# The last row of wo: sixteen DMAs of 15 rows down to 1 in place of one DMA of 128 rows

## The chip, the cores and the metric

The kernel runs on one core of a Trainium2 chip. Its five engines are named as in the profile: PE (TensorE, with PEld for its weight loads), DVE (VectorE), ACT (ScalarE), POOL (GpSimd) and SP (SyncE), beside 16 DMA engines that move data between HBM and SBUF. The metric is device time in microseconds (us) of one execution, lower is better, given as the median of several runs. Beside it there is a profile of one execution: a page, and a trace that can be asked for more.

## The reference, cut to what matters

One decoding step of a layer for 8 sequences: attention over a key and value cache, and beside it an MLP, both from the same normalised input, summed with the input.

```python
# B=8, Sq=1, D=640, Hq=Hkv=32, Sk=4096, Dh=128, F=1728; all bfloat16
def _A_ref(x, k_cache, v_cache, wq, wo):
    q = transpose((x @ wq).reshape(B, Sq, Hq, Dh), 0, 2, 1, 3)
    scores = jnp.einsum("bhqd,bhkd->bhqk", q, k_cache) * (Dh ** -0.5)
    p = _softmax(scores, axis=-1)
    o = jnp.einsum("bhqk,bhkd->bhqd", p, v_cache)
    return transpose(o, 0, 2, 1, 3).reshape(B, Sq, Hq * Dh) @ wo

def _B_ref(x, w1, b1, w2, b2):
    y = _layernorm(x)
    h = _gelu(jnp.einsum("bsd,df->bsf", y, w1) + b1)
    return jnp.einsum("bsf,fd->bsd", h, w2) + b2

xn = _layernorm(A_x)
return A_x + _A_ref(xn, ...) + _B_ref(xn, ...)
```

The two caches are 8 x 32 x 4096 x 128 elements of two bytes each, 268 MB apiece; the page counts 551.80 MB read from HBM in all. wo has 4096 rows (32 heads of 128) of 640 columns.

## The kernel before

The attention is done in 32 turns (`NQ`), one for each sequence and each group of 8 heads (`HS`). A turn loads 8 heads of the key cache and 8 of the value cache, 8 MB each, as 128 partitions with 256 keys of 128 elements. A part of the scores is computed by DVE (multiply, add, reduce), the rest by transposes and matmuls on PE; ACT does the exponentials and PE the product with V. K goes alternately to two slots of one large SBUF tensor (`S_sb`), V to a third.

Each engine's program is written down by hand: `at(pos, fn, ...)` gives every step a position, the steps are sorted by it, and each engine's calls are recorded in that order. `_Eng` records compute instructions with a semaphore, and `_Dma` counts 16 on its semaphore for each DMA, so that `sig` hands back a ticket of the semaphore and the sum so far. `_Eng.wait` waits for a ticket. On PE, DVE and ACT the turns run as loops; SP's program has no loop.

SP issues all large loads in order: wq, then K and V turn by turn, the MLP's weights w1 and w2, and at the end wo. x, b2, the rest of w2, b1 and the final store are issued by ACT. Nearly everything in the core's stream from HBM thus stands in one queue, in SP's order.

wo is loaded last, because its place in SBUF is the slot of the last odd turn's K: `load_wl` (line 382) waits until that K has been read. Its five DMAs follow one another without another wait. `load_wl(0)` brings the first half (20 KB for each partition), `load_wl(1)` the third quarter (10 KB), and `load_wn` (line 395) the last quarter in three pieces, cut at `WN_CUT = (0, 5, 7, HS)` (line 230): five of the eight rows that each partition holds, then two, then one. In the prediction these are `wn0`, `wn1` and `wn2`. A piece of one row is 640 elements, 1280 bytes, on each of 128 partitions: partition p gets row 8p + 7 of the last 1024 rows of wo. Each piece has a semaphore of its own (`ld_wn`).

At the end PE multiplies the attention output by wo into ACC_ps, an accumulator that already holds x, b2 and the MLP's result. `fin_wl` does it for the first three quarters. `fin_wn(q)` (line 766) waits for its piece of the last quarter and for the reordered output of the last heads (`oS3_sb`), and then runs five matmuls for each of its rows: 25, 10 and 5. `fin_store` (line 777) waits for the last matmul, copies ACC_ps to SBUF on DVE, transposes it on PE, evicts it on ACT and issues the store from ACT. SP's last instruction waits for that store.

The recorded instructions all go out through the helper `_emit`, so the profile gives nearly all of them line 111, and its waits line 109.

Of the kernel before, what the change touches and what calls it, by code (L numbers as in the profile page):

```python
# [14 lines left out]
P = 128  # L15
# [177 lines left out]
def bass_parallel_sum__gqa_block_cached__mixer_channel_mlp__decode_kernel(  # L193
# [13 lines left out]
    B, _, D = A_x.shape  # L207
# [3 lines left out]
    HS = 8  # L211
# [16 lines left out]
    RW = P // HW  # L228
    NL = 3
    WN_CUT = (0, 5, 7, HS)  # L230
    V_CUT = (0, 192, 256)

    def jp_of(i):
# [17 lines left out]
    with ExitStack() as es:  # L251
# [7 lines left out]
        def part(slot, lo, n, rows=P):  # L259
            return S_sb[0:rows, slot, lo:lo + n]  # L260
# [3 lines left out]
        def scratch(n, rows=P, slot=KB):  # L264
# [14 lines left out]
        woL_sb = part(KB, HW * D, 2 * HS * D).rearrange("p (g x) -> p g x", g=2)  # L279
# [58 lines left out]
        pe, dve, act, sp, pool = (_Eng(sem(f"{n}_s")) for n in ("pe", "dve", "act", "sp", "pool"))  # L338
# [3 lines left out]
            _Dma(sem(n)) for n in ("ld_x", "ld_b1", "ld_b2", "ld_wq", "ld_w1", "ld_w2a", "ld_w2b", "st_o"))  # L342
        ld_vl = [_Dma(sem(f"ld_vl{q}")) for q in range(1, len(V_CUT) - 1)]
        ld_wl = [_Dma(sem(f"ld_wl{q}")) for q in range(2)]
        ld_wn = [_Dma(sem(f"ld_wn{q}")) for q in range(len(WN_CUT) - 1)]
        tk = {}
        prog = []

        def at(pos, fn, *a):
            prog.append((pos, len(prog), fn, a))  # L350
# [21 lines left out]
        def load_v(i):  # L372
# [4 lines left out]
            tk[("v", i)] = []  # L377
            for d, lo, hi in zip([ld_s[VS]] + ld_vl, V_CUT[:-1], V_CUT[1:]):
                if lo:
# [15 lines left out]
        def load_wn(q):  # L395
            lo, hi = WN_CUT[q], WN_CUT[q + 1]
            n = HS * DH
            tk[("wn", q)] = ld_wn[q].sig(sp.dma_start(
                woL_sb[:, 1, lo * D:hi * D],
                A_wo[NL * n:(NL + 1) * n, :].rearrange("(p s) n -> p (s n)", p=P)[:, lo * D:hi * D]))  # L400

        def zero_w2b():
            tk["w2z"] = pool.sig(pool.memset(w2b_sb[:, :], 0.0))
# [264 lines left out]
        def pe_PV(i):  # L668
            PVB.use(pe)
            pe.wait(tk[("exp", i)])  # L670
            for j in range(NKEY):
                if j == 0:
                    pe.wait(tk[("v", i)][0])
                elif j in V_CUT:
                    pe.wait_ge(ld_vl[V_CUT.index(j) - 1].sem, 1)
                last = pe.matmul(PV_ps[:, 0:HS], tile[VS][:, j, :], P_sb[:, :, j],
# [89 lines left out]
        def fin_wn(q):  # L766
            lo, hi = WN_CUT[q], WN_CUT[q + 1]
            pe.wait(tk[("wn", q)], tk[("oS", 3, 0)], tk[("oS", 3, 1)])
            for r in range(lo, hi):
                for c in range(DC):  # L770
                    last = pe.matmul(ACC_ps[:, c * B:(c + 1) * B],
                                     woL_sb[:, 1, r * D + c * P:r * D + (c + 1) * P], oS3_sb[:, r, :],
                                     start=False, stop=(r == HS - 1), skip_group_check=True)
            if hi == HS:
                ACCB.used(pe, pe.sig(last))
# [73 lines left out]
        for q in range(2):  # L849
            at(o + 50 + 0.1 * q, load_wl, q)  # L850
            at(o + 79.1 + 0.2 * q, fin_wl, q)
        for q in range(len(WN_CUT) - 1):
            at(o + 51 + q, load_wn, q)
            at(o + 80 + q, fin_wn, q)
# [70 lines left out]
```

## Time and profile before

| | |
|---|---|
| Time, median of 3 runs | 1281.99 us (1281.98 to 1282.0) |
| Span of the profiled execution, first to last instruction | 1280.5 us |
| Busy: DVE | 1103.8 us (86%) |
| Busy: PE | 671.1 us (52%) |
| Busy: PE's weight loads | 573.4 us (45%) |
| Busy: ACT | 476.6 us (37%) |
| Busy: POOL | 106.3 us (8%) |
| HBM traffic over the span | 431 GB/s |
| Issue of the five DMAs of wo on SP | from 1255.97 us, 2.23 us in all |

The median is 1.5 us above the span, for what lies before the first and after the last instruction. Busy times are instruction records; the issue of a DMA, a wait and a branch do not count as busy. Times in rows are microseconds from the start of the span. The DMA row gives the busy share of the 16 DMA engines together, in tenths; "DMA share" in a table of windows is the same as a fraction. The queue q1 is SP's and q10 is ACT's; a "packet" is one record of a DMA engine, either data or the small write that reports completion. "SPq" and "ACTq" stand for the issue of a DMA by that engine.

### The profile page before, as it was taken

What the parts mean: (1) busy time and instruction counts of PE and PEld (TensorE: products, weight loads), DVE (VectorE), ACT (ScalarE), POOL (GpSimd) and SP (SyncE); (2) the same over time, 40 slices, a digit from 0 to 9 for tenths busy, and PEclk for the clock granted to TensorE, in tenths of its full rate; (3) what the DMA queues carried; (4) which work ended last, traced back from release to release, by engine and by line L of the source; (5) the groups of instructions that cost most, each with busy time, mean ns of one, the idle gap of its engine ahead of it and who ended that gap; (6) DMA issues with size and microseconds to landing.
All of it is one profiled execution on the core that took longest, in us unless ns stands there. A gap on an engine that the chain in (4) does not pass through costs nothing.

```text
span 1280.5 us, 34440 instructions
## 1 busy us (share of the span) xinstructions
PE 671.1 (52%) x13944; PEld 573.4 (45%) x13944; DVE 1103.8 (86%) x680; ACT 476.6 (37%) x904; POOL 106.3 (8%) x113
## 2 busy tenths in 40 slices
PE   1546555446545446545456554456454466464476
PEld 1435444335535345444345444345343355353365
DVE  1899999889888889888899888898888898888895
ACT  0524444233444233443234443234443234442331
POOL 0020010000000000000000000000000000000040
PEclk9755655566665565555565565566655555555655
DMA  9999999999999999999999999999999999999998
GB/s 419 431 426 435 426 436 432 442 426 436 432 440 428 434 432 438 432 432 430 436 438 426 434 434 442 426 434 434 438 430 430 430 440 436 428 432 436 433 437 361
DMA packets 10675, 551.99 MB, mean 431 GB/s; under 512 B 1244, under 2 KB 1445, under 8 KB 1702
## 3 DMA queue, kind: packets, MB, share of 16 engines
q1 hardware_dynamic: 10512, 551.70, 99.7%
q8 instruction: 9, 0.15, 0.0%
q10 hardware_dynamic: 150, 0.11, 0.0%
q14 instruction: 4, 0.03, 0.0%
HBM read 551.80 MB, written 0.01 MB: 431 GB/s over the span
## 4 chain that ended last, share of the span: by engine, by line
DMA 52%; DVE 36%; issue 11%; DVEq 0%; PE 0%; SPq 0%; ACT 0%
DMA S_sb<-in_A_k_cache_dram 51%; DVE S_sb L111 26%; DVE Sd_sb L111 8%; DMA S_sb<-in_A_wo_dram 2%; DVE S_ps L111 1%; DVE ri_sb L111 0%; DVEq L109 0%; PE ACC_ps L111 0%; DVE mx_sb L111 0%; SPq L111 0%; DVE mbT_sb L111 0%; DVE mxT_sb L111 0%; DVE mq_sb L111 0%; DVE mb_sb L111 0%; PE QB_ps L111 0%
## 5 line engine op out<-in xcount | busy, mean ns | idle before, releaser
L111 PE MATMUL TR_ps<-ident_bf,S_sb 128*128 128x128 bf16 (+1 forms) x2570 | 341.2, 273 | 354.1 <-POOL kr_sb L111 333.7
L111 DVE TENSOR_TENSOR S_sb<-S_sb,qbc_sb 128x7552 bf16<-128x7552 bf16 (+1 forms) x96 | 392.5, 4088 | 128.8 <-DMA S_sb<-in_A_k_cache_dram 128.4
L111 PEld LDWEIGHTS TR_ps<-ident_bf,S_sb 128*128 (+2 forms) x2570 | 243.6, 102 | 414.0 <-issue 338.2
L111 DVE TENSOR_REDUCE Sd_sb<-S_sb 128x59 f32<-128x3776 bf16 (+1 forms) x96 | 390.2, 4065 | 6.0
L111 ACT ACTIVATE KT_sb<-TR_ps 128x1024 bf16<-128x1024 bf16 x320 | 327.0, 1024 | 121.1 <-PE TR_ps L111 109.5
L111 PE MATMUL PV_ps<-P_sb,S_sb 128*128 128x8 bf16 x8192 | 224.0, 175 | 137.5 <-DMA S_sb<-in_A_v_cache_dram 134.5
L111 PEld LDWEIGHTS PV_ps<-P_sb,S_sb 128*128 128x128 bf16 x8192 | 221.4, 103 | 140.2 <-DMA S_sb<-in_A_v_cache_dram 137.0
L111 DVE TENSOR_TENSOR S_sb<-S_sb 128x3776 bf16<-128x3776 bf16 (+1 forms) x96 | 205.4, 2140 | 3.3
L111 ACT ACTIVATE P_sb<-Sd_sb,NB_sb 128x256 bf16<-128x256 f32 x256 | 126.3, 494 | 213.7 <-DVE NB_sb L111 213.7
L111 PE MATMUL S_ps<-qrep_sb,KT_sb 128*128 128x8 bf16 x2560 | 121.6, 177 | 51.6 <-ACT KT_sb L111 48.6
L111 ACT ACTIVATE oU_sb<-PV_ps 128x8 f32<-128x8 f32 x31 | 5.5, 178 | 376.8 <-PE PV_ps L111 376.8
L111 PEld LDWEIGHTS S_ps<-qrep_sb,KT_sb 128*128 128x128 bf16 x2560 | 91.3, 102 | 82.2 <-ACT KT_sb L111 41.6
L111 POOL TENSOR_TENSOR oT_sb<-oU_sb,ri_sb 128x8 bf16<-128x8 f32 x31 | 71.8, 2316 | 374.8 <-DVE S_sb L111 303.1
L111 POOL COPY qrep_sb<-qT_sb 128x128 bf16<-128x128 bf16 x32 | 19.2, 600 | 472.6 <-PE S_ps L111 454.0
L111 ACT ACTIVATION_READ_ACCUMULATOR P_sb<-Sd_sb,NB_sb 128x1 f32 x256 | 47.7, 186 | 0.0
L111 DVE TENSOR_TENSOR S_ps<-S_ps,mask_sb 128x320 f32<-128x320 f32 (+1 forms) x65 | 31.6, 486 | 2.6 <-PE S_ps L111 2.6
L111 DVE TENSOR_REDUCE Sd_sb<-S_ps 128x40 f32<-128x320 f32 x64 | 31.5, 492 | 2.2
L111 PE MATMUL QB_ps<-ident_bf,qrep_sb 128*128 128x128 bf16 x32 | 9.2, 286 | 40.7 <-DVE S_sb L111 21.2
L111 ACT ACTIVATE qbc_sb<-QB_ps 128x128 bf16<-128x128 f32 x32 | 8.9, 278 | 56.9 <-PE QB_ps L111 56.9
L111 POOL MEMSET kr_sb<- 128x1 f32 x32 | 3.2, 99 | 295.4 <-DMA S_sb<-in_A_k_cache_dram 295.4
L111 PEld LDWEIGHTS QB_ps<-ident_bf,qrep_sb 128*128 128x128 bf16 x32 | 3.3, 104 | 43.6 <-ACT oU_sb L111 29.3
L111 PE MATMUL CH_ps<-rs_sb,ones_f 128*128 128x8 f32 x64 | 16.7, 335 | 6.5 <-ACT P_sb L111 6.5
(73 smaller groups left out, 148.6 us busy)
## 6 DMA issues: line engine op xcount, KB each, us to landing
S_sb<-in_A_v_cache_dram SPq DMA_DIRECT2D x1, 6144.0 KB, 26.8
S_sb<-in_A_wq_dram SPq DMA_DIRECT2D x1, 5120.0 KB, 15.2
S_sb<-in_A_wo_dram SPq DMA_DIRECT2D x1, 2560.0 KB, 15.8
S_sb<-in_B_w_dram SPq DMA_DIRECT2D x1, 2160.0 KB, 30.3
S_sb<-in_B_w_dram SPq DMA_DIRECT2D x1, 2080.0 KB, 34.8
S_sb<-in_A_v_cache_dram SPq DMA_DIRECT2D x1, 2048.0 KB, 31.3
S_sb<-in_A_wo_dram SPq DMA_DIRECT2D x1, 1280.0 KB, 18.5
S_sb<-in_A_wo_dram SPq DMA_DIRECT2D x1, 800.0 KB, 20.0
```

Of the source, the lines that this page charges most:

```text
L111: inst = getattr(e, name)(*a, **k)
```

## The change

`load_wn` is changed for the piece that reaches the last row (`hi == HS`, that is `wn2`). Instead of one DMA to 128 partitions it issues sixteen, each to the next k partitions, with k from a new list, `ROWS_CUT`: 15, 14, 13, 12, 11, 10, 9, 8, 8, 7, 6, 5, 4, 3, 2, 1, which add up to 128. The other two pieces keep their one DMA of 128 partitions. Each of the sixteen adds 16 to the same semaphore; the ticket kept is that of the last, so PE's wait in `fin_wn(2)` is for 256 instead of 16. The bytes, their source and their place are the same.

```diff
     WN_CUT = (0, 5, 7, HS)
+    ROWS_CUT = (15, 14, 13, 12, 11, 10, 9, 8, 8, 7, 6, 5, 4, 3, 2, 1)
     V_CUT = (0, 192, 256)
...
         def load_wn(q):
             lo, hi = WN_CUT[q], WN_CUT[q + 1]
             n = HS * DH
-            tk[("wn", q)] = ld_wn[q].sig(sp.dma_start(
-                woL_sb[:, 1, lo * D:hi * D],
-                A_wo[NL * n:(NL + 1) * n, :].rearrange("(p s) n -> p (s n)", p=P)[:, lo * D:hi * D]))
+            src = A_wo[NL * n:(NL + 1) * n, :].rearrange("(p s) n -> p (s n)", p=P)
+            a = 0
+            for k in ROWS_CUT if hi == HS else (P,):
+                tk[("wn", q)] = ld_wn[q].sig(sp.dma_start(
+                    woL_sb[a:a + k, 1, lo * D:hi * D], src[a:a + k, lo * D:hi * D]))
+                a += k
```

On PE, DVE, ACT and POOL the program is the same. On SP one DMA of 128 x 640 elements, the last one of its queue, becomes sixteen.

## The prediction

> **What bounds the kernel now.** I read the page's busy lines first, then the chain that ended last, then its last pieces in order of time.
>
> ```profile
> span 1280.5 us, 34440 instructions
> DMA  9999999999999999999999999999999999999998
> HBM read 551.80 MB, written 0.01 MB: 431 GB/s over the span
> DMA 52%; DVE 36%; issue 11%; DVEq 0%; PE 0%; SPq 0%; ACT 0%
> ```
>
> The DMA engines are busy in every slice and the core draws 431 GB/s throughout. The kernel is a stream from HBM; the change adds no byte and moves none to an earlier place, so only the end of the stream can matter. The last pieces of the chain of waits:
>
> ```profile
> 1255.97 0.33 SPq L111
> 1256.30 0.04 issue
> 1256.34 0.43 SPq L111
> 1256.77 0.04 issue
> 1256.82 19.96 DMA S_sb<-in_A_wo_dram
> 1276.78 0.05 issue
> 1276.82 1.50 PE ACC_ps L111 x40
> 1278.33 0.02 issue
> 1278.35 0.21 DVE res_sb L111
> ```
>
> The end hangs on wo: from 1276.82 PE runs 40 matmuls into ACC_ps, then the result is copied, transposed, evicted and stored. The 40 are three groups behind three waits: 25 for the first piece of wo's last eighth (`wn0`), 10 for the second (`wn1`), 5 for the third (`wn2`, the edited DMA). Windows laid on the gaps, with the instructions that touch ACC_ps alone, show each wait (columns: stretch, length, PE busy and count, weight loads busy and count, VectorE, granted clock, DMA share, GB/s):
>
> ```profile
> 1276.81:1277.57 0.76, 0.75 (x25) 0.74 (x25) 0.00 (x0) 0.50 0.42 143
> 1277.57:1277.60 0.03, 0.03 (x4) 0.00 (x0) 0.00 (x0) 0.50 0.00 0
> 1277.60:1277.96 0.36, 0.36 (x12) 0.34 (x10) 0.00 (x0) 0.50 0.00 0
> 1277.96:1278.01 0.05, 0.05 (x3) 0.00 (x0) 0.00 (x0) 0.50 0.00 0
> 1278.01:1278.25 0.24, 0.24 (x7) 0.21 (x5) 0.00 (x0) 0.50 0.00 0
> ```
>
> The weight loads (second count) are the clean column: 25, a gap without any, 10, a gap, 5. So `wn1` lets PE go at 1277.60 and `wn2` at 1278.01. Fifteen more loads cost 0.74 - 0.34 = 0.40 us, 27 ns each. Had `wn2` been there in time, the last five would have begun ten loads after 1277.60, at 1277.87, instead of at 1278.01. **The edited DMA is thus last on the path, by 0.14 us and no more**: a gain beyond that meets `wn1`, which the change doesn't touch.
>
> Why does it land late? The DMA engines do not stop together:
>
> ```profile
> 1275.60:1276.00 0.40, 0.40 (x22) 0.40 (x18) 0.33 (x2) 0.00 (x0) 0.00 (x0) 0.50 1.00 397
> 1276.00:1276.40 0.40, 0.40 (x19) 0.40 (x15) 0.00 (x0) 0.00 (x0) 0.00 (x0) 0.50 0.80 307
> 1276.40:1276.80 0.40, 0.09 (x4) 0.00 (x0) 0.00 (x0) 0.00 (x0) 0.00 (x0) 0.50 0.76 294
> 1276.80:1277.20 0.40, 0.38 (x14) 0.38 (x15) 0.00 (x0) 0.00 (x0) 0.00 (x0) 0.50 0.67 227
> 1277.20:1277.60 0.40, 0.40 (x17) 0.36 (x14) 0.00 (x0) 0.00 (x0) 0.00 (x0) 0.50 0.18 64
> ```
>
> The DMA share (last but one) falls from 1.00 to 0.80, 0.76, 0.67 and 0.18 over 1.6 us, with no data after that. Idle share by time is 0.4 x (0.20 + 0.24 + 0.33 + 0.82) = 0.64 us on the mean engine: a perfectly even finish would bring the last byte 0.64 us forward, more than the 0.14 us that can be used.
>
> **The change, part by part.** It removes one DMA of 128 rows of 1280 bytes and adds sixteen of 1 to 15 rows, the same 160 KB, at the same place at the end of SP's queue. The wait of PE becomes one for the sum over the sixteen.
>
> *SP's issues.* Rows of issue times:
>
> ```profile
> L111 SPq DMA_DIRECT2D S_sb<-in_A_wo_dram x5: 328/432/433, 1256.0 to 1257.8; - x5
> 0.74 0.60 ACTq L111 DMA_DIRECT2D S_sb<-in_A_x_dram  x1
> 1.37 0.23 ACTq L111 DMA_DIRECT2D S_sb<-in_B_b_dram  x1
> 1279.24 0.33 ACTq L111 DMA_DIRECT2D out_dram<-out_sb  x1
> S_sb<-in_A_wo_dram SPq DMA_DIRECT2D x1, 320.0 KB, 20.3
> S_sb<-in_A_wo_dram SPq DMA_DIRECT2D x1, 160.0 KB, 20.2
> ```
>
> An issue of 1 row took 0.23 us, of 8 rows 0.60, of 40 rows 0.33, of 128 rows 0.33 to 0.43. Sixteen beginning at 1257.8 end between 1257.8 + 16 x 0.23 = 1261.5 and 1257.8 + 16 x 0.60 = 1267.4; I take 0.43, 1264.7. The old DMA was issued at 1257.8 and landed 20.2 us later, at 1278.0, because 5 MB of wo and the last of V stood ahead of it. So the issues hide behind that transfer, with over 8 us to spare; without this cover they would cost 16 x 0.43 = 6.9 us. Behind them SP has only its wait for the store, which waits for PE anyway. Cost 0.
>
> *How the rows fall on the engines.* The ACT queue shows how a short DMA is spread. x has 8 rows, and its window holds 16 packets of that queue, 8 of them small:
>
> ```profile
> DMA packets 32, 0.67 MB, mean 555 GB/s; under 512 B 8, under 2 KB 16, under 8 KB 16
> q10 hardware_dynamic: 16, 0.01, 4.6%
> q10 hardware_dynamic: 150, 0.11, 0.0%
> ```
>
> So 8 rows brought 8 completion packets, one per engine used. Over the run the ACT queue moves 8 + 1 + 1 + 64 + 40 = 114 rows in 150 packets; the 36 others fit 8 + 1 + 1 + 16 + 10, that is, 40 rows went to 10 engines and 64 to all 16. Rows go to as many engines (at most 16) as divide their number. A DMA of 15 rows then puts one row on each of 15 engines, one of 14 on 14, and the two of 8 use 8. If they always begin with the same engine, the engines get 16, 15, 14, 13, 12, 11, 10, 9, 7, 6, 5, 4, 3, 2, 1 and 0 rows, against 8 each. (The Trainium skill says the same of the number, and that HWDGE takes the lowest-numbered engines: "DMA: Bandwidth & Descriptors", section on why a DMA increments its semaphore by 16. No view names the engines.)
>
> *What that does to the finish.* A row takes 1280 B / (431/16 GB/s) = 0.048 us. The first engine gets 8 rows more, +0.38 us, the last 8 fewer, -0.38 us. An engine also writes one completion per DMA that it serves, at most 16 instead of 1. No row prices one: nothing at least, at most as much as a row, 0.048 us, so the first engine gets 0 to 15 x 0.048 = 0.72 us more. I take it near 0, since it is a tiny packet. Whether this helps depends on which engines finish late. If the first ones finish early (the share has fallen to 0.76 by 1276.8, so they have some 0.8 us of room), the late ones get less and `wn2` lands up to 0.38 us earlier, of which PE can use 0.14. If the first ones finish late, the landing is 0.38 to 1.1 us later. I take the first: descriptors are made in the order of the rows, so an engine that serves the first rows of every DMA should start and finish each of them first. That is an assumption, and its opposite is a rival.
>
> *PE, VectorE, ScalarE, GpSimd.* The instructions are the same; the five matmuls run as before, so nothing is added behind the wait.
>
> *Sum*, on the profiled execution: 1280.5 - 0.14 = 1280.4 us of span. The median of the runs is 1281.99, 1.5 us over the span, so 1281.99 - 0.14 = **1281.85 us**. Within 0.2% (2.6 us, about what a measurement of this kernel can tell from no change) this is no change.
>
> A rule of the Trainium skill speaks against: "SBUF — State Buffer", section on the DMA setup-cost knee, has every transfer pay a roughly fixed 2 us; in series fifteen more would be an estimate of 30 us. The two rows of 320 and 160 KB above disagree: issued 0.43 us apart, they landed about 0.3 us apart, so what is fixed overlaps in a full queue.
>
> **The rivals.**
>
> *Late engines get more* (0.22). The landing is 0.38 to 1.1 us late, all of it on the path: 1282.4 to 1283.1; if the late engines merely keep their rows, 1282.0. For it: nothing shows which engines are late. Against: the order of descriptors.
>
> *Neighbouring rows collide in SBUF* (0.16). The old DMA gives each engine its own eight rows; in the new ones up to 15 engines write 15 neighbouring partitions at once. If four neighbours share one way in that is no faster than one engine, a DMA of k rows lasts up to 4 x 0.048 = 0.19 us, thirteen of them 2.5 us, and the short ones of 3, 2 and 1 rows 0.29 us: 2.8 us against 8 x 0.048 = 0.38 us now. In series that is +2.4 us. Since the engines come to them up to 1.6 us apart, I take half, +1.2: 1283.2; bounds 1282.0 and 1284.4. For it: nothing in the trace. Against: the x load wrote 8 neighbouring rows in the window above without visible queueing, though only once. The Trainium skill bears this rival: the same page's section on the DMA port swizzle gives four neighbouring partitions one port of about 27 GB/s. No run here shows it.
>
> *All rows on few engines: slower* (0.06). If an odd count went to one engine (the factor shared with 16 deciding), the first would take 15+13+11+9+7+5+3+1 = 64 rows, and of the even DMAs 7+5+3+1, 3+1 and 1+1, in all 86. That is 78 x 0.048 = 3.7 us more, less up to 1.2 us of room: from 1284.5 to 1285.7. It decides as soon as 40 rows use 8 engines and not 10, but then the ACT queue would hold 148 packets, not 150.
>
> *The queue takes only a few DMAs at a time: slower* (0.05). With at most eight in flight (V, four of wo, three short ones), each landing lets one more in. When `wn1` lands at 1277.6, eight would still be unissued: 8 x 0.33 = 2.6 us of issues plus a transfer of under 1 us, against the 0.4 us that `wn2` now takes from there: about +3.0, 1285. It decides below some fifteen. Against: six stood in the queue at 1258 and the issues kept to 0.43 us; more were never tried.
>
> **How the numbers follow.** Forecast 0.51, at 1281.85 (1281.75 to 1282.0); late engines 0.22; collision 0.16; few engines 0.06; short queue 0.05. All but the last two, and a tail of the collision (0.02), stay within 0.2%: same 0.86, slower 0.13. Faster by 2.6 us cannot come from a wait worth 0.14 us: 0.01 for what I overlook. The range reaches below the forecast only by what `wn1` may move too, 1281.6, and above it over the bulk of the first two rivals, to 1283.3.
>
> **What would show it.** Right: the gap between the tenth and eleventh of PE's last fifteen weight loads is gone and the DMA share falls more steeply after 1276.4, with sixteen issues on SP done before 1268. The rivals: the gap grows to 0.5 us or more (late engines, or collision if 1280-byte packets last longer); one engine's data runs on alone for microseconds (few engines); SP's issues stretch beyond 1270 (short queue). A changed time with `wn2` landing as before, or a `wn1` that moves by over 0.1 us, would make the account wrong.

## The result, and the profile after

| | before | after |
|---|---|---|
| Median of 17 runs each, on the same chips | 1282.08 us (1281.9 to 1282.68) | 1284.59 us (1283.71 to 1285.26) |
| Span of the profiled execution | 1280.5 us | 1282.6 us |
| Start of PE's last five weight loads | 1278.01 us | 1280.1 us |

The changed kernel is slower by 2.5 us: the ratio is 1.0018, with a 95% interval of 1.0011 to 1.0025, and no run of it is as fast as any run of the kernel before. By the prediction's bar of 0.2% (2.6 us) this would still count as no change; the runs tell the two apart all the same. The forecast was 1281.85 us, the range 1281.6 to 1283.3; both missed. (The profiled execution of the changed kernel was one of its faster ones, 1283.94 us; its trace explains 2.1 us.)

The end of the chain of waits of the changed kernel (start, length, what):

```profile
1263.02 0.25 SPq L111
1263.28 0.04 issue
1263.32 16.74 DMA S_sb<-in_A_wo_dram
1280.06 0.05 issue
1280.11 0.31 PE ACC_ps L111 x5
```

The last of SP's issues begins at 1263.32 and is over by 1263.6, as the sum had it (1264.7). The DMA issued last then holds the chain for 16.74 us, and PE is released for five matmuls only. Where the time lies is seen by laying windows on PE's waits again (instructions that touch ACC_ps; columns as in the prediction, with weight loads as the second count, and DMA share and GB/s last):

```profile
1276.95:1277.72 0.77, 0.76 (x25) 0.74 (x25) 0.00 (x0) 0.50 0.39 96
1277.72:1278.06 0.34, 0.07 (x3) 0.00 (x0) 0.00 (x0) 0.50 0.04 11
1278.06:1278.43 0.37, 0.35 (x10) 0.35 (x10) 0.00 (x0) 0.50 0.00 0
1278.43:1280.10 1.67, 0.08 (x3) 0.00 (x0) 0.00 (x0) 0.50 0.00 0
1280.10:1280.35 0.25, 0.24 (x5) 0.21 (x5) 0.00 (x0) 0.50 0.00 0
```

Read the fourth row: PE waits 1.67 us for `wn2`, and in all of that time the DMA engines move nothing, 0 GB/s. In the kernel before, the same gap was 0.05 us. The second row holds a smaller wait: `wn1`, which the edit leaves alone, lets PE go at 1278.06 instead of 1277.60. That costs nothing, since `wn2` comes much later still.

The DMA engines' records end long before PE is let go. This is all that they did from 1277.6 to 1280.06 (the view gives GB/s only in the first 0.25 us of it):

```profile
DMA packets 11, 0.01 MB, mean 3 GB/s; under 512 B 6, under 2 KB 11, under 8 KB 11
```

The data is not late by the records. What comes late is the report that it has landed. The stretches on the same scale as before say so too:

```profile
1276.80:1277.20 0.40, 0.24 (x9) 0.24 (x10) 0.00 (x0) 0.00 (x0) 0.00 (x0) 0.50 0.92 217
1277.20:1277.60 0.40, 0.40 (x22) 0.40 (x19) 0.00 (x0) 0.00 (x0) 0.00 (x0) 0.50 0.19 48
1277.60:1278.00 0.40, 0.19 (x8) 0.10 (x4) 0.00 (x0) 0.00 (x0) 0.00 (x0) 0.50 0.05 16
```

Up to 1277.20 the engines are fuller than before (share 0.92 against 0.67), yet they move fewer bytes (217 GB/s against 227): more of their time goes into each byte. (By the single records: a row of 1280 bytes took 0.055 to 0.060 us before and up to 0.188 us now. All 128 together took 8.4 us instead of 7.1, under 0.1 us for each of 16 engines.) After 1277.60 one engine is left with a remainder.

The queue line shows how the rows fell on the engines:

```profile
DMA packets 10787, 551.99 MB, mean 430 GB/s; under 512 B 1356, under 2 KB 1557, under 8 KB 1814
q1 hardware_dynamic: 10624, 551.70, 99.5%
```

SP's queue had 10512 packets before, under 512 bytes there were 1244: 112 more now, all of them small. The one DMA of 128 rows had 16 completions. Sixteen DMAs on 15, 14 ... 1 engines have 15 + 14 + ... + 1 + 8 = 128, which is 112 more. The rows went as forecast, one to an engine, each with a completion of its own.

The increments of `wn2`'s semaphore stand in the trace; the last of them, in microseconds from the start of the span:

```
before: 1277.576 1277.682 1277.755 1277.765 1277.775 1277.876 1277.913 1277.971
after:  1279.403 1279.456 1279.553 1279.605 1279.659 1279.862 1280.064
```

Before, the last eight of the sixteen reports come in within 0.4 us (all sixteen within 1.5 us). The last record of SP's queue ends at 1277.54, 0.43 us ahead of the last report. After, that record ends at 1277.90. At that moment 84 of the 128 reports are still to come, the last of them 2.17 us later, and the tail is a series with a step of 0.20 us (1279.456, 1279.659, 1279.862, 1280.064). That step made the theory for the experiments.

### The profile page after: what moved, and what is told of

It is laid out like the page before. It is cut to its first block, busy times and chain, and to the rows that moved or that the text cites. A ratio compares the mean times of both kernels' runs of the same rounds, so it can differ in the third digit from the quotient of the medians.

```text
span 1282.6 us, 34455 instructions
## 1 busy us (share of the span) xinstructions
PE 670.0 (52%) x13944; PEld 572.1 (45%) x13944; DVE 1103.6 (86%) x680; ACT 476.2 (37%) x904; POOL 106.5 (8%) x113
## 4 chain that ended last, share of the span: by engine, by line
DMA 52%; DVE 36%; issue 11%; SPq 1%; DVEq 0%; PE 0%; ACT 0%
DMA S_sb<-in_A_k_cache_dram 51%; DVE S_sb L111 26%; DVE Sd_sb L111 7%; DVE S_ps L111 1%; DMA S_sb<-in_A_wo_dram 1%; SPq L111 1%; DVE ri_sb L111 0%; DVEq L109 0%; DVE mx_sb L111 0%; DVE mbT_sb L111 0%; DVE mxT_sb L111 0%; DVE mq_sb L111 0%; DVE mb_sb L111 0%; PE ACC_ps L111 0%; PE QB_ps L111 0%
```

## The experiments

Three theories. **C**: an engine's completions are confirmed one after another, some 0.2 us each, so that many short DMAs on one engine end long after their data. **N**: rows of neighbouring partitions, written together, collide on their way into SBUF. **U**: the finish is uneven and the engine with most rows was a late one anyway. All kernels compute the whole result. Each was timed against the kernel before on the same chip, 11 runs each; the ratios' 95% intervals are about 0.0009 to either side of the ratio, since they allow for the spread of the kernel before, so the ranges of the runs are given where they say more.

**The same rows with 3 completions or with 19.**

```diff
-    ROWS_CUT = (15, 14, 13, 12, 11, 10, 9, 8, 8, 7, 6, 5, 4, 3, 2, 1)
+    ROWS_CUT = (96, 15, 17)             # one17
+    ROWS_CUT = (96, 15) + (1,) * 17     # singles17
```

> wn2 as three DMAs: 96 rows (6 on each of 16 engines), 15 rows (one on each of 15) and 17 rows, which one engine takes alone. That engine moves 24 rows with 3 completions. Theory C (an engine's completions are confirmed one after another, about 0.20 us each): 16 rows more at 0.055 us are 0.9 us on an engine, two completions more 0.4 us; PE's last five matmuls begin between 1278.0 (if this engine is an early one) and 1279.3; time +0.0 to +1.3 us against before. Theory N (neighbouring rows collide on their way into SBUF): one engine alone cannot collide, only the 15 rows can, +0.0 to +0.2. Theory U (the engine with most rows was late anyway, and rows are all that counts): +0.9.

> The same as one17, but the 17 rows are seventeen DMAs of one row: the same rows on the same engine, with 19 completions instead of 3. Theory C: seventeen confirmations in a row, 17 x 0.20 = 3.4 us after the engine's own data; PE's last five begin at about 1280.4, time about +2.4 us against before, 1.5 to 2.5 us above one17. Theories N and U: the same as one17 within 0.2 us, since rows, partitions and engine are the same.

Measured: one17 1282.59 us against 1282.06 (+0.5; ratio 1.0005, 0.9996 to 1.0014), singles17 1284.05 us (+2.0; ratio 1.0016, 1.0007 to 1.0025). Their runs do not overlap: 1282.26 to 1283.46 and 1283.82 to 1285.02. Splitting 17 rows of one engine into 17 DMAs, with nothing else changed, costs 1.5 us, at the lower end of what C said (1.5 to 2.5); N and U gave no difference. In the profile of singles17, taken of its slowest run (1285.02 us; windows on ACC_ps), the wait is as empty as in the changed kernel:

```profile
1278.60:1278.95 0.35, 0.00 (x0) 0.00 (x0) 0.00 (x0) 0.50 0.04 4
1278.95:1281.17 2.22, 0.00 (x0) 0.00 (x0) 0.00 (x0) 0.50 0.00 0
```

PE waits 2.22 us beside DMA engines that move nothing.

**Whose queue is it, the engine's or the semaphore's?** All these completions count on one semaphore, so its increments might be what stands in line.

```diff
-        tk[("wn", q)] = ld_wn[q].sig(...)          # one semaphore for all 19
+        tk[("wn", q)].append(ld_wx[x].sig(...))    # sems17: one for each
```

> singles17 with a semaphore of its own for each of the 19 DMAs of wn2; PE waits for all of them. Theory C (the engine confirms its completions one after another): as singles17, +1.7 to +2.4 us against before. Theory S (increments of one semaphore hold each other up): the seventeen completions overlap, +0.2 to +0.8 us, like one17.

Measured: 1284.13 us against 1282.05, +2.1 (ratio 1.0016, 1.0007 to 1.0025), the same as singles17. The semaphore is not it. Since each DMA of one row now has its own, the trace gives each landing by itself (microseconds, in the order of issue):

```
1277.265 1277.441 1277.616 1277.790 1277.975 1278.159 1278.340 1278.520 1278.697
1278.874 1279.050 1279.223 1279.408 1279.591 1279.773 1279.953 1280.131
```

Sixteen steps in 2.866 us, 0.179 us each, and no step is under 0.17 or over 0.19. The record of such a row is 0.055 us long in the kernel before. The last record of SP's queue ends at 1278.08, 2.05 us before the last landing: the engines do not hold back the rows, the reports stand in line behind them.

**Completions without foreign rows or unevenness.** wn2 cut by columns: each DMA still covers all 128 partitions, and every engine has the same eight.

```diff
+            m = 8 if hi == HS else 1     # cols8; cols4 has 4, cols2 has 2
+            cw = (hi - lo) * D // m
+            for c in range(lo * D, hi * D, cw):
+                tk[("wn", q)] = ld_wn[q].sig(sp.dma_start(woL_sb[:, 1, c:c + cw], src[:, c:c + cw]))
```

> wn2 as eight DMAs of 128 partitions and 80 columns (160 bytes): each engine writes only its own eight partitions as before, evenly, but with 8 completions instead of 1 and 64 small packets instead of 8. Theory C: seven confirmations more behind the latest engine's data, +1.0 to +1.6 us. Theory N: no collision, only the smaller packets, +0.2 to +0.5. Theory U: even, +0.0 to +0.5.

> wn2 as four DMAs of 128 partitions and 160 columns, each engine in its own partitions: four completions per engine. Theory C: a quarter of the data takes about 0.11 us and a confirmation about 0.2 us, so the confirmations set the end: 4 x 0.2 = 0.8 us instead of the 0.42 us that the data took, +0.3 to +0.6 us, between cols2 (0.0) and cols8 (+1.55). A fixed cost per DMA would give about +0.66 (three sevenths of cols8), and then also +0.2 for cols2.

> wn2 as two DMAs of 128 partitions and 320 columns: two completions per engine instead of one, evenly, each engine in its own eight partitions. Theory C with its price of about 0.2 us: the second half of the data takes about 0.2 us itself, so the second confirmation hardly waits for the first, 0.0 to +0.15 us. If every DMA more cost a fixed amount at the end, +0.2 or more.

Measured: cols8 1283.61 against 1282.06 us (+1.55; 1.0012, 1.0003 to 1.0021), cols4 1282.61 against 1282.10 (+0.51; 1.0004, 0.9995 to 1.0013), cols2 1282.05 against 1282.06 (0.0; 1.0, 0.9991 to 1.0009). Two, four and eight completions an engine cost 0.0, 0.5 and 1.55 us by the medians; the interval of cols4 taken alone includes no change, that of cols8 does not. A fixed price for a DMA does not give this curve; confirmations of 0.2 us that run beside the data do: two hide behind the 0.4 us that the data takes anyway, each further one shows. (From four to eight the step is 0.26 us each. The packets of cols8 are small too, 160 bytes, so its surplus isn't all confirmation.)

**Neighbours, or not.** Eight DMAs of 16 rows, either of 16 neighbouring partitions or of every eighth.

```diff
+    ROWS_CUT = (16,) * 8                                   # near16
...
+            for i in range(8) if hi == HS else (None,):    # far16
+                r = slice(i, P, 8 if hi == HS else 1)
+                tk[("wn", q)] = ld_wn[q].sig(sp.dma_start(
+                    woL_sb[r, 1, lo * D:hi * D], src[r, lo * D:hi * D]))
```

> wn2 as eight DMAs of 16 neighbouring rows: 8 rows and 8 completions on every engine, no unevenness; 16 engines write 16 neighbouring partitions together. Theory C: the same number of completions as cols8, +1.2 to +1.7 us. Theory N: collisions on top or alone; if alone +1.1, if on top of C +2 or more.

> near16 with the rows of each DMA eight partitions apart (i, i+8, i+16 ...): the same rows, DMAs and completions, no neighbours. Theory C: as near16 within 0.3 us, +1.2 to +1.7 us. Theory N: 0.5 us or more below near16.

Measured: near16 1283.75 us, far16 1283.82 us, before 1282.05 us: +1.70 (1.0012, 1.0003 to 1.0022) and +1.77 (1.0013, 1.0004 to 1.0022). Neighbours or not makes no difference, so N as it stood falls. Both are close to cols8 with the same eight completions an engine. Their last waits, near16 first, then far16:

```profile
1278.60:1279.74 1.14, 0.00 (x0) 0.00 (x0) 0.00 (x0) 0.50 0.00 0
```

```profile
1278.90:1279.80 0.90, 0.00 (x0) 0.00 (x0) 0.00 (x0) 0.50 0.00 0
```

**Foreign partitions.** With two DMAs, where confirmations hide, cutting by rows can be set against cutting by columns.

```diff
+    ROWS_CUT = (64, 64)     # half64
```

> wn2 as two DMAs of 64 rows: again two completions and eight rows per engine, but each engine writes partitions that in the DMAs of 128 belong to others, beside engines that are still busy with wn1. Theory C alone: as cols2, 0.0 to +0.15 us. With a cost for writing among others' partitions (theory N in a weaker form: the 2560-byte packets of wn1 get longer): +0.3 to +0.6 us.

Measured: 1282.51 against 1282.06 us, +0.45 (1.0004, 0.9995 to 1.0013), where cols2 had 0.0; the runs are 1282.14 to 1282.91 and 1281.87 to 1282.14, while half64's interval alone includes no change. So something else than the number of completions seems to cost about 0.45 us when a DMA of fewer rows gives the engines other partitions than one of 128 (here four rows for each engine, out of half the partitions). The traces show it in the records. The rows of `wn1`, 2560 bytes, which are the same in all kernels, took at most 0.114 us in the kernel before and in cols2, cols4 and cols8. In half64 their median is 0.113 us and the longest 0.156, and all other kernels whose wn2 is cut by rows at the end have such long records too (longest 0.147 to 0.224 us, far16's the longest). So records last longer wherever wn2 is cut by rows at the end, neighbours or not; why, and whether that is all of the 0.45 us, stays open. (In half64 the longer records of `wn1` and `wn2` add up to 0.16 us for each engine, and its profiled execution was its fastest, 1282.14 us.)

**From the last record to the last report.** The traces together, in microseconds. The second column is counted by the rule for the spread of rows; the third is the end of the last record of SP's queue.

| run | completions on the fullest engine | last record ends | last landing of wn2 | between |
|---|---|---|---|---|
| before | 1 | 1277.54 | 1277.97 | 0.43 |
| cols2 | 2 | 1277.73 | 1278.18 | 0.44 |
| half64 | 2 | 1277.84 | 1278.26 | 0.42 |
| one17 | 3 | 1278.44 | 1278.95 | 0.51 |
| cols4 | 4 | 1277.79 | 1278.52 | 0.73 |
| cols8 | 8 | 1277.86 | 1279.36 | 1.50 |
| near16 | 8 | 1277.78 | 1279.71 | 1.93 |
| far16 | 8 | 1278.24 | 1279.77 | 1.54 |
| after | 16 | 1277.90 | 1280.06 | 2.17 |
| singles17 | 19 | 1278.92 | 1281.13 | 2.22 |

The records, small ones of the completions included, end at about the same time whether an engine reports once or eight times (far16's half a microsecond later). What grows with the number of completions is the time from there to the last report. (one17 and singles17, with 24 rows on one engine, end later.) The 0.45 us of half64 is not in this column.

**Are the first engines early?**

```diff
+    ROWS_CUT = (120, 8)     # probe; a semaphore for each
```

> wn2 as two DMAs, 120 rows (8 on each of 15 engines) and 8 rows (one on each of 8 engines), each with a semaphore of its own, so that the landings tell which engines are late: the one engine without a row of wn2, and the eight with a row of the short DMA. If the first engines are early (the forecast's assumption): the eight landings of the short DMA come before the last of the 120 rows, -0.1 to +0.1 us. If they are late: the short DMA's land last, one row and one completion, +0.2 to +0.4 us.

Measured: 1282.66 against 1282.05 us, +0.6 (1.0004, 0.9995 to 1.0013). The landings in the trace:

```
120 rows, 15 engines: 1276.873 1276.937 1277.016 1277.113 1277.384 1277.401 1277.516
                      1278.063 1278.073 1278.102 1278.148 1278.199 1278.208 1278.363 1278.396
8 rows, 8 engines:    1277.122 1277.228 1277.288 1277.588 1277.595 1277.691 1278.303 1278.597
```

The interval includes no change. Seven engines land early and eight late, with a gap of half a microsecond between. Of the eight that served the short DMA six are early, two are late, and the last landing of all, 1278.597, is one of theirs, 0.201 us after the last of the 120 rows. If a short DMA goes to the first engines, as the prediction had it (no view names them), its assumption holds in this trace for six of the first eight and fails for the two that count: they are late and get more.

**The sixteen DMAs earlier in the queue.** If the trouble is at the end alone, it should go when other transfers follow.

```diff
-            at(o + 51 + q, load_wn, q)
+            at(o + 51 + q if q < 2 else o + 50.05, load_wn, q)
```

> The changed kernel's sixteen DMAs, but issued before wl1, wn0 and wn1 instead of last, so that wn1 ends the stream. Theory C, if later data flows past unconfirmed completions: the 3 us of confirmations lie beside 7 us of transfers, PE ends on wn1's ten matmuls, -0.2 to +0.2 us against before; if they hold up the engine's queue, about +2. Theory N: the collisions cost as much as at the end, since the stream sets the time: +0.3 to +2. Theory U: +0.4 or less.

Measured: 1283.75 against 1282.06 us, +1.7 (1.0014, 1.0005 to 1.0023). It doesn't go. The windows where the sixteen DMAs pass, in this kernel and then in the kernel before (second trace, `again`):

```profile
1270.00:1272.00 2.00, 2.00 (x81) 2.00 (x78) 0.00 (x0) 0.00 (x0) 0.00 (x0) 0.50 1.04 292
1272.00:1274.00 2.00, 1.70 (x65) 1.63 (x62) 0.19 (x1) 0.00 (x0) 0.00 (x0) 0.50 0.95 331
```

```profile
1270.00:1272.00 2.00, 2.00 (x81) 2.00 (x79) 0.00 (x0) 0.00 (x0) 0.00 (x0) 0.50 0.96 405
1272.00:1274.00 2.00, 1.70 (x64) 1.64 (x62) 0.19 (x1) 0.00 (x0) 0.00 (x0) 0.50 1.00 420
```

The engines count as busy and move 292 and 331 GB/s instead of 405 and 420: 2 us x (113 + 89) GB/s = 0.40 MB not moved, 0.9 us of the stream. The large packets behind are slowed: rows of 10240 bytes took 0.385 to 0.396 us in the kernel before and up to 0.975 us here. Whether the completions slow them or the foreign partitions do, as in half64, no run separates. The last DMA here is also `wn1`, whose ten matmuls follow its landing instead of five (0.13 us). The rest of the 1.7 us isn't accounted for.

**The kernel before, again.**

> The kernel before, unchanged, for its own spread and a second trace: 0.0 us, within 0.2. wn0 and wn1 let PE go at 1276.8 and 1277.6 as in the first trace if these do not vary; a shift of 0.2 us or more would say that small shifts of them in the other traces mean nothing.

Measured: 1282.04 against 1282.06 us (1.0, 0.9991 to 1.0009). In its second trace the chain of waits reads:

```profile
1277.00 1.50 PE ACC_ps L111 x40
```

PE starts at 1277.00 where the first trace had 1276.82: single traces of one kernel differ by 0.2 us here, so nothing was concluded from shifts of that size.

## Why the prediction was wrong

- *The place.* Right: the edited DMA is last on the path, and the time is lost in PE's last wait. But `wn1` moved as well: it let PE go 0.46 us later than in the first trace and landed 0.27 us later than in the second (1278.03 against 1277.76), where the prediction allowed 0.1. Records that last longer, as in half64, fit this; it stays hidden behind `wn2`. (The prediction's "last eighth" of wo is its last quarter; nothing hangs on that.)
- *SP's issues, cost 0.* Right: the twenty issues were over by 1263.6.
- *How the rows fall.* Right in number, by the 112 packets more.
- *The price of a completion.* **This is the step that failed.** The sum had bounded it by 0.048 us, a row's time, and took it near 0 "since it is a tiny packet". A packet's record is short, but the confirmations of one engine come 0.18 to 0.20 us apart, 0.179 us in sems17. The bound came from the nearest row by size, and what limits a completion isn't size. The step includes its row, so with the measured price sixteen steps take 2.9 to 3.2 us on the first engine. Before, its eight rows and one completion took about 0.4 us from the landing of `wn1` to that of `wn2`. That is 2.5 to 2.8 us more, in place of the sum's 0.38 us for rows and 0 to 0.72 for completions, less what the engine had in hand for finishing early; the trace shows 2.1 us. What hid the price before is seen in cols2: with 0.2 us of data for each completion, confirmations keep up. A hint stood in the prediction's own windows: the DMA engines moved nothing from 1277.57 on, yet `wn2` let PE go only at 1278.01.
- *Which engines are late.* Half right: six of the first eight are early, the other two are late and get more rows. The gain of 0.14 us was out of reach for this alone; probe, with one row and one completion more on eight engines, was already 0.6 us slower by the medians, though part of that can be the foreign partitions. That descriptors are made in the order of the rows, the reason given for the choice, no run shows.
- *The rivals.* Late engines get more: the direction was right, the price, 0.38 to 1.1 us, had the same false bound on completions in it. Collision of neighbours: refuted by near16 and far16. Its sign, that 1280-byte packets last longer, did come (up to 0.188 us instead of 0.060), but the records of wn2 grew by under 0.1 us for each engine, and foreign partitions cost about 0.45 us in half64, not 2.5. All rows on few engines, and a queue that takes few DMAs: they named times near the measured one, 1284.5 to 1285.7, but the 112 packets refute the first, and the issues, which never stretched, the second.

The rule of the Trainium skill that the prediction set aside ("SBUF — State Buffer", section on the DMA setup-cost knee: about 2 us for every transfer) is still not what the traces show: cols2 has a DMA more and costs nothing. Nearer is "DMA: Bandwidth & Descriptors", section on queues, rings and completion order: the increment of the semaphore is a strongly ordered write that lands only after every earlier write of that engine. Increments that alternate with rows would then each wait for their row to be confirmed. The steps of sems17 agree, but no run separates the wait for the row from the increment itself. The same page's anatomy of one DMA, told for the SWDGE path, calls the write to the semaphore essentially free and puts most of the fixed cost on the confirmation that the data has landed. The 0.18 us steps can be such confirmations in a row; whether they are, no run shows.

Not settled: the 0.4 us between the 2.1 us of the profiled execution and the 2.5 us of the medians, what a confirmation spends its 0.18 us on, and why records last longer in the kernels cut by rows.

## What to carry to other kernels

At the end of a stream, count the completions that one DMA engine must report, not only its bytes: here up to one in 0.2 us came free beside the data, and each beyond it took its engine about 0.2 us (in the kernel's time 0.26 us each from cols4 to cols8, 0.09 us each from one17 to singles17). A DMA may be cut in two by columns at no cost here (0.0 us), but cutting to even out the last half microsecond cost more than there was to win. A price bounded by the nearest row in size holds only if size is what limits it; for an operation whose record is short, look at when its effect arrives.

## What had not been expected of the hardware

A series of short DMAs by rows holds up the data behind it: in `early` the engines' records stayed busy while the rate fell to 292 GB/s. And SP's queue does have a limit, which the changed kernel doesn't reach. The issue times of wo's DMAs (shortest, median, longest in ns; first and last start) of cols8 and then of singles17:

```profile
L111 SPq DMA_DIRECT2D S_sb<-in_A_wo_dram x12: 328/432/5253, 1255.9 to 1272.0; - x12
```

```profile
L111 SPq DMA_DIRECT2D S_sb<-in_A_wo_dram x23: 229/262/2206, 1256.1 to 1268.5; - x23
```

One issue of cols8 took 5.25 us and one of singles17 2.2 us, while the sixteen of the changed kernel took at most 0.49 us. What the limit counts stays open. In packets on the fullest engine, wo's first four DMAs are 4 x (8 + 1) = 36, and the changed kernel adds 16 x 2 = 32, 68 in all, none held. But cols4 adds 4 x 9 = 36, 72 in all, and none is held either, while singles17 is first held at its thirteenth single row, at 36 + 7 + 2 + 13 x 2 = 71. So a plain count of packets gives no single limit. The stalls ended before the data did, and PE's end did not hang on them.
